# Where weight loads, weight conversions and the second batch's first loads stand in the order of a Fourier filter and mixture-of-experts kernel

## The chip, the cores and the metric

The kernel runs on one core of a Trainium2 chip. The metric is the device time in microseconds (us), lower is better. Three runs of the kernel before took 1503.29, 1506.89 and 1511.69 us, so the median is 1506.89 us.

## The reference

A batch of 8 sequences (2496 x 256, float32) is filtered in the frequency domain, and each of the 19968 filtered rows goes through the one of 8 experts that its router picks:

```python
X = np.fft.rfft(x, axis=1)
y = np.fft.irfft(X * (filt_r + 1j * filt_i)[None], n=2496, axis=1)      # 8 x 2496 x 256
xn = y / (norm(y) + 1e-6);  en = emb / (norm(emb) + 1e-6)               # rows, experts
logits = xn @ en.T / tau;   e = argmax(logits);   gate = softmax(logits)[e]
out = gate * (relu(y @ w1[e]) @ w2[e])                                  # w1: 256 x 1024, w2: 1024 x 256
```

## The kernel before, in words

**The filter.** Each of the 8 batches is a group. Its transform of length 2496 = 64 x 39 is done by matmuls in four steps, each a Python generator: `conv_s1` (products `s1_g_t`, 11 tiles, stored to the DRAM buffer SD), `conv_s2` (loads `a` from SD, products `s2_g_k`, 10 tiles; VectorE multiplies by the filter tiles `f` into `yy` and `xs`, GpSimd adds the two; product `sa_g_j`; store to ZD), and `conv_sb` (loads from ZD, products `y`, 11 tiles, quantised to two float16 halves in `rows`, transposed as `tp`, router logits `lp`). `route` counts ranks with matmuls `rk`, and 22 indirect DMAs per batch (line 767) scatter the rows to the DRAM buffer XS, sorted by expert.

**The slots.** A `Slot` is a block of up to 256 rows of one expert; slot `0_e` is that of batch 0 and expert e. SyncE (SP) loads its rows transposed (`xT`, line 890) and their index and gate (`meta`). Then, for each of four quarters `fp`, `up` runs 12 matmuls into `ph` (line 921), ScalarE (ACT) writes the ReLU as the upper float16 half of `h` (line 927), VectorE (DVE) writes the lower half (line 928), and `down`, two quarters later, runs 12 matmuls into `po` (line 948). There are two buffers for `ph`, so quarter n+2 waits for the lower half of quarter n. A block of 12 matmuls, up or down, is called a block below.

**The weights.** An expert's float32 weights come in four pieces of 128x1024 (w1 in two, w2 in two), loaded by `weight_load`, 1 MB per DMA. Before use DVE takes the maximum of each piece (`wmx`, line 251), two small matmuls (`pm`, lines 262 and 266) with DVE work between make the scale `wsc`, and each piece is scaled and split into two float16 halves: ACT 286 and 287 with GpSimd 288 for the first piece, ACT 290 with DVE 291 for the others. Before slot `0_e` can start, all of w1 of expert e must be converted.

**What sets the order.** The front of the program, through batch 0's router, stands in the order in which it is written. After that, each engine's order is chosen at build time by a list scheduler that goes by its own estimates of time; the engines then run their lists strictly in order. `behind(name)` is the kernel's handle on it: an instruction issued under it may not be placed ahead of the one that `last[name]` holds. Before the change `last` knows "sum", "sp" (the latest slot's `meta` load), "pe" and "dve". The slots of batch g run while `conv_s2` and `conv_sb` of batch g+1 and `conv_s1` of batch g+2 are worked off between their blocks. All the weights are loaded and converted before or during the slots of batch 0.

Of the kernel before, what the change touches and what calls it, by code (L numbers as in the profile page):

```python
# [57 lines left out]
def moe_spectral_kernel(  # L58
# [154 lines left out]

    def weight_load(q, e, j):

        w = (w1, w2)[j]
        if e + 1 < E:
            raw = W32[:, e + 1, j * 2048:(j + 1) * 2048]
            q.dma_start(raw, w[:, e])
            raws[e, j] = [[raw[:, i * 1024:(i + 1) * 1024]] for i in range(2)]  # L220
        elif j == 0:
            raw = W32[:, e, 2048:4096]
            q.dma_start(raw, w[:, e])
            raws[e, j] = [[raw[:, i * 1024:(i + 1) * 1024]] for i in range(2)]
        else:
            raw = W32[:, e, 2048:3072]
            q.dma_start(raw, w[:, e, 1024:2048])
            small = []
            for i in range(2):
                t = mp2.tile([P, 512], F32, tag="wp", name=f"wraw{i}")  # L230
                q.dma_start(t, w[:, e, i * 512:(i + 1) * 512])
                small.append(t)
            raws[e, j] = [small, [raw]]
# [10 lines left out]
    def weight_halves():  # L244
# [3 lines left out]
        def largest(e, j):  # L248
            pieces = raws[e, j][0] + raws[e, j][1]
            for i, r in enumerate(pieces):  # L250
                v.tensor_reduce(out=wmx[:, i:i + 1], in_=r, axis=AX.X, op=ALU.max, apply_absolute_value=True)  # L251
            v.tensor_reduce(out=wmax[:, e, j:j + 1], in_=wmx[:, :len(pieces)], axis=AX.X, op=ALU.max)

        def spread_max(e, js):
# [23 lines left out]
        def halves(e, j):  # L278
            sc = wsc[:, e, j // 2:j // 2 + 1]
            pieces = raws[e, j // 2][j % 2]  # L280
            w = 1024 // len(pieces)
            for i, raw in enumerate(pieces):
                hi = W[:, e, j * 2048 + i * w:j * 2048 + (i + 1) * w]
                lo = W[:, e, j * 2048 + 1024 + i * w:j * 2048 + 1024 + (i + 1) * w]
                if j == 0:
                    nc.scalar.activation(raw, raw, AF.Copy, scale=sc)
                    nc.scalar.copy(hi, raw)
                    nc.gpsimd.tensor_tensor(out=lo, in0=raw, in1=hi, op=ALU.subtract)
                else:
                    nc.scalar.activation(hi, raw, AF.Copy, scale=sc)  # L290
                    v.scalar_tensor_tensor(out=lo, in0=raw, scalar=sc, in1=hi, op0=ALU.mult, op1=ALU.subtract)

        def maxima(e):
# [146 lines left out]
    def load_f(g, k):  # L440
        nb = GROUPS[g]
        fts = []
        for k2 in range(k * 2 // nb, (k + 1) * 2 // nb):
            if g:
                ft = cf.tile([P, 2, D], F32, tag="f", name=f"f{g}_{k2}")
            else:
                ft = W32[:, E - 3:].rearrange("p e c -> p (e c)")[:, k2 * CW:(k2 + 1) * CW]
                ft = ft.rearrange("p (r c) -> p r c", r=2)
            (nc.scalar if g == 1 and k < 2 else nc.sync).dma_start(ft, filt[k2])
            fts.append((k2, ft))  # L450
        return fts

# [26 lines left out]
    def conv_s2(g):  # L479
# [5 lines left out]

        def load_a(k):
            at = cin.tile([P, CW], F32, tag="in", name=f"a{g}_{k}")
            (nc.scalar if g == 1 and k < INB - 1 else nc.sync).dma_start(at, sd[:, k])
            return at

        def filtered(out_, in_, fts, ri):
# [371 lines left out]
    def behind(engine):  # L863
        return tc.issue_after(last[engine].ins) if engine in last else ExitStack()

    class Slot:
# [45 lines left out]
        def up(self, fp, between=None):  # L912
# [4 lines left out]
            for fi in range(2):  # L917
                c = 0
                for k in range(2):
                    for wh, xh in ((0, 0), (0, 1), (1, 0)):  # L920
# [3 lines left out]
                        if between and fi * 6 + c == MID:  # L924
                            between()
            h = mp3.tile([P, 2, 2, 256], F16, tag="h", name=f"h{nm}_{fp}")
            nc.scalar.activation(h[:, 0, :, :size], ph[:, :, :size], AF.Relu)  # L927
            hd = nc.vector.scalar_tensor_tensor(out=h[:, 1, :, :size], in0=ph[:, :, :size], scalar=0.0,  # L928
                                           in1=h[:, 0, :, :size], op0=ALU.max, op1=ALU.subtract)
            self.hs.append(h)  # L930
            if fp == 2:
                gate = self.meta[:, :, 1]
# [229 lines left out]
```

## Time and profile before

| | |
|---|---|
| median of three runs | 1506.89 us |
| time of the profiled execution | 1503.04 us |
| its span, first to last instruction | 1501.3 us |
| mean granted TensorE clock | 0.923 of full |
| TensorE busy | 1299.1 us, 87% |
| VectorE busy | 874.5 us, 58% |
| ScalarE busy | 694.8 us, 46% |
| GpSimd busy | 556.0 us, 37% |

Busy time is the time in which an engine had an instruction at work; it is an average over stages with different limits. The change bears on one stage, from the end of batch 0's router (about 133 us into the span) to the first matmul of batch 1's slots (about 345 us), so the rows further down are read there.

### The profile page before, as it was taken

The numbers are of one execution on the slowest core, as the hardware profiler recorded it, in microseconds if no ns is written. First come the engines' busy times: TensorE is split into PE (matmuls) and PEld (weight loads), VectorE is DVE, ScalarE is ACT, GpSimd is POOL, SyncE is SP. The second block draws the span as 40 slices with busy tenths as digits, with TensorE's granted clock in tenths as the row PEclk, the third lists the DMA queues.
The fourth block names the chain that finished last, engine by engine and source line by source line (L and its number), as shares of the span: only waits on it lengthen the run. The fifth ranks groups of instructions, "written<-read, shape, count | busy, mean of one in ns | idle before, by whom it ended". The sixth has DMA issues, their size and how long they took to land.

```text
span 1501.3 us, 32031 instructions
## 1 busy us (share of the span) xinstructions
PE 1299.1 (87%) x10972; PEld 990.7 (66%) x10972; DVE 874.5 (58%) x2870; ACT 694.8 (46%) x1578; POOL 556.0 (37%) x621
## 2 busy tenths in 40 slices
PE   5563599869898988899989988999899689999998
PEld 2132376546666756686678666867787568899997
DVE  2478967754465746575656555755577342266665
ACT  3451567535544744465346534653466122333333
POOL 1325234443344424542444244524531451122222
PEclk7875699989999999999999998999999889999999
DMA  9778657447756574657466746674664222122221
GB/s 294 252 230 271 201 180 208 137 155 201 186 138 173 178 177 131 183 178 197 129 189 185 190 107 182 182 190 128 182 175 104 77 82 54 42 57 48 48 45 40
DMA packets 229958, 229.15 MB, mean 153 GB/s; under 512 B 125867, under 2 KB 171915, under 8 KB 227870
## 3 DMA queue, kind: packets, MB, share of 16 engines
q1 hardware_dynamic: 199900, 150.10, 37.9%
q0 software_dynamic: 26592, 60.28, 13.0%
q10 hardware_dynamic: 3298, 16.64, 3.2%
q8 instruction: 92, 1.51, 0.4%
q14 instruction: 76, 0.62, 0.1%
HBM read 121.61 MB, written 84.84 MB: 138 GB/s over the span
## 4 chain that ended last, share of the span: by engine, by line
PE 61%; issue 15%; DVE 7%; DMA 7%; ACT 4%; POOL 4%; another core or an unknown queue 2%; SPq 0%; POOLq 0%; ACTq 0%; DVEq 0%
PE ph L921 20%; PE po L948 20%; PE s L431 5%; PE y L431 5%; POOL out_dram L956 3%; PE tp L658 3%; DMA ZD<-z 2%; PE s L436 2%; PE sa L436 2%; DMA f<-ZD 2%; PE sa L431 2%; DVE wmx L251 1%; PE lp L673 1%; DMA in<-in_x 1%
## 5 line engine op out<-in xcount | busy, mean ns | idle before, releaser
L948 PE MATMUL po<-W,h 128*128 128x256 f16 (+1 forms) x3864 | 523.9, 280 | 29.5 <-issue 15.8
L948 PEld LDWEIGHTS <-h 128*128 128x128 f16 x3864 | 376.6, 100 | 135.6 <-issue 83.1
L921 PE MATMUL ph<-xT,W 128*128 128x256 f16 x3072 | 415.1, 281 | 20.2 <-issue 9.3
L928 DVE SCALAR_TENSOR_TENSOR h<-ph,h 128x512 f16<-128x512 f32 (+1 forms) x388 | 231.3, 597 | 270.0 <-ACT h L927 226.8
L921 PEld LDWEIGHTS <-W 128*128 128x128 f16 x3072 | 304.2, 101 | 113.7 <-issue 72.9
L927 ACT ACTIVATE h<-ph 128x512 f16<-128x512 f32 (+1 forms) x388 | 203.2, 526 | 353.0 <-PE ph L921 204.3
L956 POOL DMA_INDIRECT out_dram<-o,meta x161 | 170.0, 1056 | 383.0 <-ACT o L955 329.2
L767 POOL DMA_INDIRECT XS<-rows,ixi x176 | 173.6, 986 | 163.3 <-issue 122.3
L537 POOL TENSOR_TENSOR yy<-yy,xs 128x512 f32<-128x512 f32 x80 | 107.2, 1342 | 205.4 <-DVE xs L500 121.3
L431 PE MATMUL y<-f,csb_sb 120*128 120x512 f32 (+1 forms) x192 | 102.9, 622 | 30.5 <-DMA f<-ZD 29.6
L391 POOL DMA_DIRECT2D in<-in_x x84 | 65.2, 781 | 149.1 <-PE s L431 112.5
L431 PE MATMUL s<-in,c_sb 117*128 117x512 f32 (+1 forms) x192 | 103.4, 634 | 12.2 <-DMA in<-in_x 6.7
L623 ACT ACTIVATE rows<-y 128x256 f16<-128x256 f32 x176 | 66.1, 384 | 91.7 <-PE y L431 85.3
L921 PE MATMUL ph<-xT,wp 128*128 128x128 f16 x1584 | 104.9, 219 | 0.1
L921 PEld LDWEIGHTS <-wp 128*128 128x128 f16 x1584 | 96.6, 98 | 2.8 <-issue 0.3
L474 ACT COPY s<-s 128x512 f32<-128x512 f32 x88 | 51.6, 587 | 99.0 <-PE s L431 45.3
L955 ACT ACTIVATE o<-po,meta 128x256 f32<-128x256 f32 x161 | 69.7, 475 | 56.8 <-PE po L948 33.3
L593 DVE SCALAR_TENSOR_TENSOR rows<-y,rr,rows 128x256 f16<-128x256 f32 x176 | 77.0, 476 | 27.6 <-ACT rows L590 26.1
L909 DVE COPY wp<-W 128x1024 f16 x132 | 62.1, 471 | 46.0 <-PE ph L921 44.1
L590 ACT ACTIVATE rows<-y,rr 128x256 f16<-128x256 f32 x176 | 73.8, 475 | 32.0 <-DVE rr L628 24.9
L498 DVE TENSOR_TENSOR yy<-s,f 128x256 f32<-128x256 f32 x140 | 52.8, 417 | 53.9 <-ACT xs L531 47.6
L658 PEld LDWEIGHTS <-rows 128*128 128x128 f16 x704 | 49.8, 100 | 40.5 <-issue 36.2
(184 smaller groups left out, 1427.5 us busy)
## 6 DMA issues: line engine op xcount, KB each, us to landing
f<-in_filt SPq DMA_DIRECT2D x136, 256.0 KB
ZD<-z SPq DMA_DIRECT2D x80, 256.0 KB
a<-SD SPq DMA_DIRECT2D x77, 256.0 KB
SD<-s SPq DMA_DIRECT2D x80, 240.0 KB
f<-ZD SPq DMA_DIRECT2D x80, 240.0 KB
in<-in_x POOLq DMA_DIRECT2D x70, 234.0 KB
W<-in_w ACTq DMA_DIRECT2D x14, 1024.0 KB
W<-in_filt SPq DMA_DIRECT2D x20, 256.0 KB
```

The costliest lines, as they stand in the source:

```text
L431: nc.tensor.matmul(out_, c[:a.shape[0]], a, start=True, stop=True)
L537: last["sum"] = nc.gpsimd.tensor_tensor(out=yy, in0=yy, in1=xs, op=ALU.add)
L590: nc.scalar.activation(rows[:, i, 0:D], y[:, i], AF.Copy, scale=rr[:, u:u + 1])
L593: nc.vector.scalar_tensor_tensor(out=rows[:, i, D:2 * D], in0=y[:, i], scalar=rr[:, u:u + 1], in1=rows[:, i, 0:D], op0=ALU.mult, op1=ALU.s ...
L658: nc.tensor.transpose(tp[:, i, j], rows[:, i, j * P:(j + 1) * P], ident)
L767: i = nc.gpsimd.indirect_dma_start(out=XS, out_offset=bass.IndirectOffsetOnAxis(ap=ix, axis=0), in_=src, in_offset=None)
L921: last["pe"] = nc.tensor.matmul(ph[:, fi, :size], wp[:, k * 2 + wh, fi * P:(fi + 1) * P], xT[:, xh * 2 + k], start=(c == 0), stop=(c == 5))
L927: nc.scalar.activation(h[:, 0, :, :size], ph[:, :, :size], AF.Relu)
L928: hd = nc.vector.scalar_tensor_tensor(out=h[:, 1, :, :size], in0=ph[:, :, :size], scalar=0.0, in1=h[:, 0, :, :size], op0=ALU.max, op1=ALU. ...
L948: nc.tensor.matmul(self.po[:, s], self.hs[fp][:, hh, fi, s * P:(s + 1) * P], self.Wp[:, off + wh * 1024:off + wh * 1024 + D], start=(fp == ...
L955: nc.scalar.activation(o, self.po[:, s], AF.Copy, scale=self.meta[:, s, 1:2])
L956: i = nc.gpsimd.indirect_dma_start(out=out, out_offset=bass.IndirectOffsetOnAxis(ap=self.meta[:, s, 0:1].bitcast(I32), axis=0), in_=o, in_ ...
```

## The change

Two more instructions are remembered in `last`: each ReLU as "relu" and each lower half as "lower". In the part that the scheduler orders, a weight load on ACT's queue, and the first ACT operation of each converted piece, may no longer be placed ahead of the latest slot's latest ReLU at the point where it is written; the maxima of the weight pieces not ahead of the latest lower half; the last expert's loads on SP, and batch 1's first loads of filter tiles and of SD, not ahead of the latest slot's `meta` load. Batch 1's first four filter loads and first three SD loads move from ACT's queue to SP's.

```diff
@@ -213,6 +213,11 @@
 
     def weight_load(q, e, j):
 
+        with behind("relu" if q is nc.scalar else "sp"):
+            loaded(q, e, j)
+
+    def loaded(q, e, j):
+
         w = (w1, w2)[j]
         if e + 1 < E:
             raw = W32[:, e + 1, j * 2048:(j + 1) * 2048]
@@ -248,7 +253,8 @@
         def largest(e, j):
             pieces = raws[e, j][0] + raws[e, j][1]
             for i, r in enumerate(pieces):
-                v.tensor_reduce(out=wmx[:, i:i + 1], in_=r, axis=AX.X, op=ALU.max, apply_absolute_value=True)
+                with behind("lower"):
+                    v.tensor_reduce(out=wmx[:, i:i + 1], in_=r, axis=AX.X, op=ALU.max, apply_absolute_value=True)
             v.tensor_reduce(out=wmax[:, e, j:j + 1], in_=wmx[:, :len(pieces)], axis=AX.X, op=ALU.max)
 
         def spread_max(e, js):
@@ -283,11 +289,13 @@
                 hi = W[:, e, j * 2048 + i * w:j * 2048 + (i + 1) * w]
                 lo = W[:, e, j * 2048 + 1024 + i * w:j * 2048 + 1024 + (i + 1) * w]
                 if j == 0:
-                    nc.scalar.activation(raw, raw, AF.Copy, scale=sc)
+                    with behind("relu"):
+                        nc.scalar.activation(raw, raw, AF.Copy, scale=sc)
                     nc.scalar.copy(hi, raw)
                     nc.gpsimd.tensor_tensor(out=lo, in0=raw, in1=hi, op=ALU.subtract)
                 else:
-                    nc.scalar.activation(hi, raw, AF.Copy, scale=sc)
+                    with behind("relu"):
+                        nc.scalar.activation(hi, raw, AF.Copy, scale=sc)
                     v.scalar_tensor_tensor(out=lo, in0=raw, scalar=sc, in1=hi, op0=ALU.mult, op1=ALU.subtract)
 
         def maxima(e):
@@ -446,7 +454,8 @@
             else:
                 ft = W32[:, E - 3:].rearrange("p e c -> p (e c)")[:, k2 * CW:(k2 + 1) * CW]
                 ft = ft.rearrange("p (r c) -> p r c", r=2)
-            (nc.scalar if g == 1 and k < 2 else nc.sync).dma_start(ft, filt[k2])
+            with behind("sp" if g == 1 else ""):
+                nc.sync.dma_start(ft, filt[k2])
             fts.append((k2, ft))
         return fts
 
@@ -485,7 +494,8 @@
 
         def load_a(k):
             at = cin.tile([P, CW], F32, tag="in", name=f"a{g}_{k}")
-            (nc.scalar if g == 1 and k < INB - 1 else nc.sync).dma_start(at, sd[:, k])
+            with behind("sp" if g == 1 else ""):
+                nc.sync.dma_start(at, sd[:, k])
             return at
 
         def filtered(out_, in_, fts, ri):
@@ -924,9 +934,10 @@
                         if between and fi * 6 + c == MID:
                             between()
             h = mp3.tile([P, 2, 2, 256], F16, tag="h", name=f"h{nm}_{fp}")
-            nc.scalar.activation(h[:, 0, :, :size], ph[:, :, :size], AF.Relu)
+            last["relu"] = nc.scalar.activation(h[:, 0, :, :size], ph[:, :, :size], AF.Relu)
             hd = nc.vector.scalar_tensor_tensor(out=h[:, 1, :, :size], in0=ph[:, :, :size], scalar=0.0,
                                            in1=h[:, 0, :, :size], op0=ALU.max, op1=ALU.subtract)
+            last["lower"] = hd
             self.hs.append(h)
             if fp == 2:
                 gate = self.meta[:, :, 1]
```

The instructions and their number are the same, apart from the queue of those seven loads. Their order differs from the end of batch 0's router until the first slots of batch 1, and not after. Line numbers of the changed kernel are 5 to 11 higher for the same statement.

**SP's queue at the end of the front.** `s1_10` is the last store of batch 1's first step, `wraw` are pieces of the last expert's w2, `a1` loads of batch 1 from SD, `f1` its filter tiles, `xT0_0` the first slot's rows. Before:

```order
L476 DMA SD1_179<-s1_10_1181 40x256
L231 DMA wraw0_2611<-in_w2 128x512
L231 DMA wraw1_2613<-in_w2 128x512
L488 DMA a1_3_1362<-SD1_179 128x512
L488 DMA a1_4_1405<-SD1_179 128x512
L890 DMA_TRANSPOSE xT0_0_1252<-XS_194 128x4x256
L892 DMA meta0_0_1254<-XS_194 128x2x2
```

And after:

```order
L485 DMA SD1_179<-s1_10_1181 40x256
L900 DMA_TRANSPOSE xT0_0_1252<-XS_194 128x4x256
L902 DMA meta0_0_1254<-XS_194 128x2x2
L458 DMA f1_0_1276<-in_filt 128x512
L458 DMA f1_1_1278<-in_filt 128x512
L458 DMA f1_2_1280<-in_filt 128x512
L458 DMA f1_3_1282<-in_filt 128x512
L498 DMA a1_0_1295<-SD1_179 128x512
```

The first slot's rows now stand ahead of all of `f1`, `a1` and `wraw`, where they stood behind two `wraw` and two `a1`.

**DVE around the first slot's lower halves.** `h0_0_n` on line 928 (938 after) is the lower half of quarter n; `wmx` on line 251 (257 after) is the maximum of a weight piece, 291 a conversion. Before:

```order
L251 TENSOR_REDUCE wmx_177<-W_170 128x1 x2
L274 RECIPROCAL winv_176<-wsc_175 128x2
L291 SCALAR_TENSOR_TENSOR W_170<-W_170,wsc_175 128x1024
L252 TENSOR_REDUCE wmax_172<-wmx_177 128x1
L276 TENSOR_TENSOR isc_171<-winv_176 128x1
L291 SCALAR_TENSOR_TENSOR W_170<-W_170,wsc_175 128x1024
L258 TENSOR_SCALAR wmax_172<-wmax_172 128x2
L251 TENSOR_REDUCE wmx_177<-W_170 128x1 x2
L291 SCALAR_TENSOR_TENSOR W_170<-W_170,wsc_175 128x1024
L928 SCALAR_TENSOR_TENSOR h0_0_0_1269<-ph0_0_0_1256,h0_0_0_1269 128x512
L259 TENSOR_SCALAR wmax_172<-wmax_172 128x2
L928 SCALAR_TENSOR_TENSOR h0_0_1_1345<-ph0_0_1_1301,h0_0_1_1345 128x512
```

And after:

```order
L797 SCALAR_TENSOR_TENSOR bad0_1246<-thr_165,adm0_1244 128x16
L800 TENSOR_SCALAR drop0_1248<-bad0_1246 128x16
L938 SCALAR_TENSOR_TENSOR h0_0_0_1269<-ph0_0_0_1256,h0_0_0_1269 128x512
L257 TENSOR_REDUCE wmx_177<-W_170 128x1 x2
L938 SCALAR_TENSOR_TENSOR h0_0_1_1345<-ph0_0_1_1301,h0_0_1_1345 128x512
L938 SCALAR_TENSOR_TENSOR h0_0_2_1392<-ph0_0_2_1379,h0_0_2_1392 128x512
L945 TENSOR_TENSOR meta0_0_1254<-meta0_0_1254,isc_171 128x2
L258 TENSOR_REDUCE wmax_172<-wmx_177 128x1
L948 TENSOR_TENSOR meta0_0_1254<-meta0_0_1254,drop0_1248 128x2
L257 TENSOR_REDUCE wmx_177<-W_170 128x1 x2
L938 SCALAR_TENSOR_TENSOR h0_0_3_1467<-ph0_0_3_1454,h0_0_3_1467 128x512
L258 TENSOR_REDUCE wmax_172<-wmx_177 128x1
```

Before, 22 maxima and nine conversions on line 291 since the end of the router stand ahead of the first lower half; after, none does. All maxima and conversions of experts 1, 2 and 3 now follow it.

**TensorE around the scale of expert 5.** `pm5_0` on line 266 (272 after) is the second small matmul for expert 5's scale. Before, it stands in the up block of slot `0_3`, two slots ahead of the one that needs it:

```order
L921 MATMUL ph0_3_2_2166<-xT0_3_1860,W_170 128x256
L921 LDWEIGHTS W_170
L921 MATMUL ph0_3_2_2166<-xT0_3_1860,W_170 128x256
L266 MATMUL pm5_0_1797<-wdg_174,one32_144 128x2
L921 LDWEIGHTS W_170
L921 MATMUL ph0_3_2_2166<-xT0_3_1860,W_170 128x256
```

After, it stands in the last down block of slot `0_4`:

```order
L959 MATMUL po0_4_2597<-W_170,h0_4_3_2667 128x256
L272 MATMUL pm5_0_1797<-wdg_174,one32_144 128x2
L959 LDWEIGHTS h0_4_3_2667
L959 MATMUL po0_4_2597<-W_170,h0_4_3_2667 128x256
L959 LDWEIGHTS h0_4_3_2667
L959 MATMUL po0_4_2597<-W_170,h0_4_3_2667 128x256
```

and these rows follow a few matmuls later, with expert 5's own slot already among them:

```order
L272 MATMUL pm6_0_1943<-wdg_174,one32_144 128x2
L439 MATMUL s1_2_0_1971<-in2_0_1963,c1_sb_117 128x512
L439 MATMUL s1_2_1_2048<-in2_1_1965,c1_sb_117 128x512
L931 LDWEIGHTS W_170
L931 MATMUL ph0_5_0_2737<-xT0_5_2416,W_170 128x256
L931 LDWEIGHTS W_170
L931 MATMUL ph0_5_0_2737<-xT0_5_2416,W_170 128x256
L931 LDWEIGHTS W_170
L931 MATMUL ph0_5_1_2837<-xT0_5_2416,W_170 128x256
L931 LDWEIGHTS W_170
L931 MATMUL ph0_5_1_2837<-xT0_5_2416,W_170 128x256
L439 MATMUL y1_0_1955<-f1_0_1897,csb_sb_120 128x512
```

The scale of expert 5 thus moved from two slots ahead of its use to half a block and four products ahead of it, and the first four matmuls of slot `0_5` (those that need no lower weight half) are drawn ahead of `y1_0`. At the end of the stage, the rank matmul `rk1_4` has 87 matmuls of slots `0_6` and `0_7` (27 `ph` and 60 `po`) between it and `rk1_8` before, and none after: they now stand ahead of it. On GpSimd the output stores of slots `0_6` and `0_7` now stand ahead of the scatters that follow `rk1_4` (eight) and `rk1_8` (six); before, only those of `0_5` stood ahead of the eight.

## Rows read from the trace of the kernel before

**Rows 1.** The page: the span, and busy time of TensorE and VectorE.

```profile
span 1501.3 us, 32031 instructions
...
PE 1299.1 (87%) x10972; PEld 990.7 (66%) x10972; DVE 874.5 (58%) x2870; ACT 694.8 (46%) x1578; POOL 556.0 (37%) x621
```

**Rows 2.** Busy time by stretch: from:to, length, each engine, TensorE clock, DMA share, GB/s.

```profile
133.50:165.70 32.20, 5.85 (x21) 2.66 (x22) 30.96 (x78) 11.57 (x12) 14.46 (x15) 0.50 0.94 344
...
165.70:205.80 40.10, 33.78 (x199) 22.88 (x199) 31.17 (x69) 20.81 (x31) 12.62 (x10) 0.85 0.57 157
205.80:250.00 44.20, 42.58 (x305) 30.73 (x304) 29.92 (x59) 33.38 (x59) 23.02 (x21) 1.00 0.66 192
250.00:287.00 37.00, 36.02 (x314) 25.49 (x313) 33.16 (x134) 23.43 (x70) 12.55 (x19) 1.00 0.62 163
287.00:345.00 58.00, 39.73 (x277) 25.34 (x276) 25.37 (x114) 17.36 (x33) 28.79 (x30) 0.82 0.46 144
```

**Rows 3.** SP in order of time: start, length (with waits inside a run), what was issued.

```profile
142.07 19.93 SPq L488 DMA_DIRECT2D a<-SD  x2
162.10 1.35 SPq L890 DMA_TRANSPOSE xT<-XS  x1
...
341.18 1.24 SPq L890 DMA_TRANSPOSE xT<-XS  x1
```

**Rows 4.** Waits of SP's queue, 130 to 170 us: total, times, longest.

```profile
SPq L488 <- PE s L431: 13.0, 1, 13.0
```

**Rows 5.** GpSimd in order of time, in brackets the idle time before.

```profile
146.97 0.90 POOL L767 DMA_INDIRECT XS<-rows,ixi  x1 [0.30 <-issue]
...
235.21 2.44 POOL L288 TENSOR_TENSOR W<-W 128x1024 f16<-128x1024 f32 x1 [3.48 <-ACT W L287]
...
310.20 0.99 POOL L767 DMA_INDIRECT XS<-rows,ixi  x1 [0.30 <-issue]
...
337.40 0.91 POOL L767 DMA_INDIRECT XS<-rows,ixi  x1 [0.30 <-issue]
```

**Rows 6.** TensorE in order of time.

```profile
165.74 5.19 PE L921 MATMUL ph<-xT,W 128*128 128x256 f16 x24 [1.96 <-DMA xT<-XS]
...
204.94 1.02 PE L431 MATMUL s<-a,c_sb 128*128 128x512 f32 x2
...
228.64 0.38 PE L266 MATMUL pm<-wdg,one 2*128 2x2 f32 x2
...
306.67 0.19 PE L738 MATMUL rk<-oh,lt 128*128 128x64 f16 x1
...
344.88 2.56 PE L921 MATMUL ph<-xT,W 128*128 128x256 f16 x22
```

**Rows 7.** VectorE in order of time.

```profile
136.35 2.34 DVE L251 TENSOR_REDUCE wmx<-W 128x1 f32<-128x1024 f32 x2
...
149.97 0.21 DVE L272 TENSOR_SCALAR wsc<-wsc 128x1 f32<-128x1 f32 x2 [0.56 <-DVE wmax L252]
...
178.49 0.68 DVE L928 SCALAR_TENSOR_TENSOR h<-ph,h 128x512 f16<-128x512 f32 x1
```

**Rows 8.** VectorE's maxima from 133 to 165.7 us, grouped: busy, mean ns.

```profile
L251 DVE TENSOR_REDUCE wmx<-W 128x1 f32<-128x1024 f32 x18 | 21.0, 1206 | 0.0
```

**Rows 9.** ScalarE in order of time.

```profile
150.16 1.15 ACT L286 ACTIVATE W<-W,wsc 128x1024 f32<-128x1024 f32 x1 [18.00 <-DVE wsc L272]
...
154.33 1.03 ACT L287 CAST W<-W 128x1024 f16<-128x1024 f32 x1
...
191.04 0.60 ACT L927 ACTIVATE h<-ph 128x512 f16<-128x512 f32 x1 [0.18 <-PE ph L921]
```

**Rows 10.** The chain that ended last, in order of time: start, length, what.

```profile
213.08 1.31 PE ph L921 x12
...
216.02 0.86 PE s L431 x2
...
311.69 8.59 another core or an unknown queue
```

## The prediction

> **What bounds the kernel now.** I read the page first: TensorE is busy 87% of the 1501.3 us span, VectorE 58% [rows 1]. Such a kernel gets faster only where TensorE stands idle, so I cut the stage in which the two orders differ into stretches [rows 2]; the reader is to compare TensorE's and VectorE's columns. From 133.5 to 165.7 us TensorE works 5.85 of 32.20 us while VectorE works 30.96. From 165.7 to 205.8 TensorE has 33.78 of 40.10. From 205.8 to 287 it is nearly full (42.58 of 44.20, 36.02 of 37.00). From 287 to 345 it has 39.73 of 58.00. The hole in front is the prize; the two full stretches are where anything pushed out of the hole must find room; the last stretch is batch 1's router.
>
> Why the hole? SP issues the first slot's rows at 162.10, behind two `a1` loads that held its queue for 19.93 us from 142.07 [rows 3], 13.0 of them for a product on line 431 that had to free the buffer [rows 4]. The first `ph` matmul starts 3.64 us after the issue, at 165.74 [rows 6]. The last scatter, which that load needs, was over at 146.97 + 0.90 = 147.87 [rows 5]. So the rows waited 14 us for their place in a queue. VectorE did not waste the time: it began the first maxima at 136.35 [rows 7], and 18 of them took 21.0 us [rows 8].
>
> **The change, part by part.** I sum against the profiled execution's 1503.04 us.
>
> *A. The rows' load goes ahead of `a1`, `f1` and `wraw`.* In batch 1 the same load is issued at 341.18 [rows 3], the last scatter ending at 337.40 + 0.91 = 338.31 [rows 5]: 2.87 later. The same after 147.87 gives 150.7, plus 3.64 gives a first matmul at 154.4 against 165.74: **-11.3**. The seven loads that go from ScalarE's queue to SP's cost no time of their own as I see it: the DMA engines were 0.94 busy in the hole, 0.57 in the next stretch [rows 2], and the products that need them now come at about 181 (below). Were they later than that, those products would wait and not the rows, which now stand ahead of them.
>
> *B. Maxima behind the first lower half.* 24 matmuls took 5.19 us [rows 6], so the first 12 are over 2.6 after 154.4; the ReLU is 0.60 [rows 9], the lower half 0.68 [rows 7]: 158.3. Expert 1's maxima, which began at 136.35, begin 22.0 us later. Ahead of its scale now stand five pairs of maxima at 2.34 (11.7), two more lower halves (1.4) and the small operations and matmuls of the scale, for which I allow 2.2: about 173.6, against 149.97 [rows 7].
>
> *C. Conversions behind ReLUs.* From the scale, ScalarE took from 150.16 to 155.36 to write its halves [rows 9]: 5.2, so 179; GpSimd's lower half is up to 2.44 more [rows 5]: 181. Slot `0_1` needs all of it for its third matmul; I put that at 182 and the block's ReLU, which also stands behind a conversion for expert 2, at 187. Before, that ReLU came at 191.04 [rows 9]. So of the 11.3 us only 4 are left here. Slot `0_0`, its 96 matmuls done from 154.4, is over at about 167.6, and TensorE then stands idle for some 11 us, apart from a few small matmuls: a new hole in place of the old.
>
> The rest I count in TensorE work done by 205.8, walking the new order with these durations. A slot matmul is 1.31 / 12 = 0.109, a pair of products 0.86 [rows 10]. Before: 175 slot matmuls (19.1) and 11 pairs (9.5), 28.6. After: 205 (22.4) and 7 pairs (6.0), 28.4. So by 205.8 the gain has been paid back: **A + B + C = 0**. Bounds: -11.3 (the preparation never waits) and +6 (the new hole also throws the clock back, below).
>
> *D. VectorE's debt.* It lost 22.0 us of work. Free on it were 1.2 us in the first stretch and 8.9 in the second [rows 2]. So at 205.8 it is 11.9 us behind. From 205.8 to 250 it has 14.3 free, from 250 to 287 only 3.8. The debt fits, but in gaps of which not all can be used, and a late lower half holds back the `ph` buffer. Nothing in the trace prices that; bounds are 0 (all in gaps) and +11.9 (none). I take **+2**, nearer the first, since the free time exceeds the debt.
>
> *E. Expert 5's scale just in time.* Before, `pm5` ran at 228.64 [rows 6], and the first piece's GpSimd half, from 235.21, ended 2.44 later at 237.65 [rows 5]: 9.0 us from matmul to ready weights. In the new order there stand between that matmul and the third of slot `0_5` ten slot matmuls (1.1), four pairs (3.4) and `pm6` at 0.38 and some: 5.1. So TensorE waits up to 3.9; ScalarE may be there a little earlier, so **+3**, bounds 0 and 3.9. Everything else in TensorE's order stands behind that wait.
>
> *F. The end of the stage.* Before, `rk1_4` ran at 306.67 and the first `ph` of batch 1 at 344.88 [rows 6]. After, 27 `ph` and 60 `po` of the last two slots stand ahead of `rk1_4`: 87 x 0.109 to 0.12 = 10 us, so 317 if nothing earlier had moved. From there the path is GpSimd's: 2.2 to the first operation, two stores and 14 scatters, each 0.99 + 0.30 [rows 5], 20.6; then 2.87 to the load; and 344.88 - 341.18 = 3.7 to the matmul: 29.4, so 346.4. That is **+1**. It rests on the patch in which slot matmuls crept, 8.59 us that the chain gives to an unknown queue [rows 10], no longer costing, since the slots are done when the scatters come. If it comes back elsewhere, the term is +8, so bounds 0 and +8.
>
> Sum: 0 + 2 + 3 + 1 = +6, so 1509. The profiled execution is 3.85 us under the median of the three runs (1503.29 to 1511.69); for a median I add half of that: **1511**. One run in three differs from another by 0.5%, so less than 0.5% (7.5 us) I call no change.
>
> **The rivals.**
>
> *The gain stays (faster).* If the preparation is not what slot `0_1` waits for, the 11.3 us stay and D to F fit into gaps: 1503.04 - 11.3 + 2 = 1494. For it: the hole is TensorE's largest. Against: VectorE was 30.96 of 32.20 busy there, with work that has to be done anyway. It decides where expert 1's scale stands before 167 rather than 173.6, or that ReLU before 180.
>
> *VectorE becomes the bound (slower).* None of the 11.9 us of debt finds a gap, since gaps come where VectorE waits for ReLUs: 1503.04 + 11.9 + 3 + 1 + 2 = 1521. For it: the last full stretch has only 3.8 free. Against: the stretch before has 14.3. It decides where VectorE is over 95% busy from 205 to 250 and TensorE falls visibly below 42.58 of 44.20.
>
> *The rows gain nothing.* Were the scatters' data to land late, near 160, the load could not be issued much earlier than 162.10, and the preparation would be late all the same: 11.3 + 6 + 2 on top, 1522. Batch 1's 2.87 us speak against it.
>
> *The clock is paid for twice.* The granted clock was 0.50 in the first stretch and 0.85 in the second, in which TensorE had just begun to work [rows 2]; 24 matmuls took 5.19 there [rows 6], 12 take 1.31 later [rows 10]. The second stretch so lost 0.15 x 40.1 = 6.0 us. If the new hole after slot `0_0` sends the clock down to 1.2 GHz again, that ramp comes once more: 1517. The Trainium skill, "TensorE: Matmul & The Clock Gate", section "What's actually happening", has the low clock as the default state, which activity lifts. By that rule the new hole would cost a ramp of its own, as the first stretch did here; no row shows such a hole in the middle of the slots.
>
> **How the numbers follow.** Forecast (no change, 1511, its own range 1502 to 1515) 0.43; gain stays 0.22; VectorE 0.22; clock 0.08; rows gain nothing 0.05. The forecast's mass above 1514.4 is about 0.05 and below 1499.4 about 0.01, and some of the gain's mass falls within the bound, so faster 0.22, same 0.40, slower 0.38. For the range I reach to the gain at 1494 and past VectorE's case to 1524; half of the gain's chance and a little above are left out.
>
> **What would show it.** A: the rows' load at 151 and the first `ph` near 154. B and C: the first lower half near 158, expert 1's first conversion near 174, TensorE idle from 168 to 179. D: VectorE over 75% from 205 to 287. E: a wait of 3 us inside slot `0_5`'s first block. F: the first `ph` of batch 1, which the two traces share from there on, 6 us later than 344.88. I am wrong if that matmul comes earlier than 340 (the debt found room after all) or later than 352.

## The result, and the profile after

The changed kernel takes 1519.47 us, the median of 20 runs (1508.73 to 1525.67), against 1506.63 us for the kernel before (20 runs, 1499.20 to 1511.69): a ratio of 1.0084, with a 95% interval of 1.0067 to 1.0101. It is slower by 0.84%, some 13 us. The profiled execution has a span of 1518.4 us, 17.1 more than before [rows 1].

Most of that arises in the stage that the prediction looked at. Its trace comes to the start of the stage, the last rank matmul of batch 0's router, 2.6 us later than the trace of before, in a part where the two orders are the same (in all the traces of this document that matmul lies between 133.5 and 136.9 us, and at 134.1 in a second trace of the changed kernel). So some 14 us belong to the stage, close to the 13 of the medians. Before, then after:

```profile
133.45 0.22 PE L738 MATMUL rk<-oh,lt 128*128 128x48 f16 x1 [2.10 <-DVE mv L728]
```

```profile
136.01 0.22 PE L748 MATMUL rk<-oh,lt 128*128 128x48 f16 x1 [2.11 <-DVE ixi L770]
```

The page, and the stage by the same stretches as before [rows 2] (from:to, length, busy time of TensorE, its weight loads, VectorE, ScalarE, GpSimd, then the granted clock, DMA share and GB/s):

```profile
span 1518.4 us, 32037 instructions
...
PE 1308.9 (86%) x10972; PEld 992.8 (65%) x10972; DVE 880.2 (58%) x2870; ACT 694.6 (46%) x1578; POOL 560.3 (37%) x621
```

```profile
133.50:165.70 32.20, 11.56 (x83) 8.87 (x83) 10.62 (x41) 3.12 (x6) 12.10 (x14) 0.58 0.65 146
165.70:205.80 40.10, 25.26 (x144) 15.52 (x141) 38.40 (x71) 24.96 (x32) 14.62 (x8) 0.79 0.79 210
205.80:250.00 44.20, 43.18 (x295) 30.81 (x296) 38.60 (x80) 24.35 (x41) 17.87 (x15) 0.96 0.60 194
250.00:287.00 37.00, 28.45 (x193) 18.34 (x192) 26.65 (x58) 23.82 (x51) 14.78 (x17) 0.91 0.68 196
287.00:345.00 58.00, 46.50 (x392) 32.12 (x391) 40.28 (x197) 26.49 (x67) 25.59 (x32) 0.91 0.44 128
```

In the hole, TensorE has twice its work (11.56 us for 5.85) and VectorE a third (10.62 for 30.96). In the next stretch it is the other way round: VectorE 38.40 of 40.10, TensorE 25.26 for 33.78. Then the surprise: from 250 to 287 us, where both engines were nearly full before, TensorE falls to 28.45 of 37.00 and VectorE to 26.65. In 287 to 345 TensorE catches up (392 matmuls for 277).

The start of the stage: GpSimd's last scatter and SP's load of the rows, then TensorE in order of time (in brackets the idle time before, and what ended it):

```profile
149.50 0.89 POOL L777 DMA_INDIRECT XS<-rows,ixi  x1 [0.30 <-issue]
...
151.67 1.34 SPq L900 DMA_TRANSPOSE xT<-XS  x1
```

```profile
154.93 5.28 PE L931 MATMUL ph<-xT,W 128*128 128x256 f16 x24 [18.53 <-DMA xT<-XS]
...
164.17 3.98 PE L959 MATMUL po<-W,h 128*128 128x256 f16 x35
168.83 0.38 PE L268 MATMUL pm<-ident,wmax 128*2 128x128 f32 x2 [0.67 <-DVE wmax L265]
...
179.64 1.03 PE L931 MATMUL ph<-xT,W 128*128 128x256 f16 x4 [0.63 <-ACT W L294]
182.87 0.59 PE L268 MATMUL pm<-ident,wmax 128*2 128x128 f32 x2 [2.20 <-DVE wsc L278]
183.39 2.07 PE L439 MATMUL s<-a,c_sb 128*128 128x512 f32 x2
185.26 3.15 PE L931 MATMUL ph<-xT,W 128*128 128x256 f16 x17
```

And the place where it loses most, on TensorE and then on ScalarE and GpSimd (line 293 to 295 are the conversion of a first piece, 298 that of the others, 565 the copy of a filter product on its way to ZD):

```profile
252.23 0.38 PE L272 MATMUL pm<-wdg,one 2*128 2x2 f32 x2
...
255.16 0.38 PE L272 MATMUL pm<-wdg,one 2*128 2x2 f32 x2 [0.62 <-DVE wdg L270]
256.66 1.13 PE L439 MATMUL s<-in,c_sb 117*128 117x512 f32 x2 [1.12 <-DVE wsc L273]
258.54 1.13 PE L439 MATMUL s<-in,c_sb 117*128 117x512 f32 x2 [0.75 <-ACT z L565]
259.50 0.60 PE L931 MATMUL ph<-xT,W 128*128 128x256 f16 x4
264.65 2.08 PE L439 MATMUL y<-f,csb_sb 120*128 120x512 f32 x2 [4.55 <-DMA f<-ZD]
266.52 3.47 PE L931 MATMUL ph<-xT,W 128*128 128x256 f16 x17
```

```profile
253.03 1.15 ACT L293 ACTIVATE W<-W,wsc 128x1024 f32<-128x1024 f32 x1 [2.07 <-DVE wsc L278]
254.08 3.21 ACT L298 ACTIVATE W<-W,wsc 128x1024 f16<-128x1024 f32 x3
257.20 0.81 ACT L966 ACTIVATE o<-po,meta 128x256 f32<-128x256 f32 x2
257.91 0.57 ACT L565 COPY z<-sa 128x512 f32<-128x512 f32 x1
258.38 1.05 ACT L294 CAST W<-W 128x1024 f16<-128x1024 f32 x1
...
262.23 2.15 POOL L295 TENSOR_TENSOR W<-W 128x1024 f16<-128x1024 f32 x1
```

Expert 5's scale comes at 252.23, and its weights are whole at 262.23 + 2.15 = 264.38. The last product of the filter's second step, copied at 257.91 behind four conversions, has yet to go through ZD before `y1_0` can start at 264.65. TensorE's idle time in these rows is 0.62 + 1.12 + 0.75 + 4.55 = 7.0 us, and what follows it runs at the lower clock (0.50 granted from 264.5 to 267 us): a pair of `y` in 2.08 us.

The end of the stage:

```profile
333.38 0.19 PE L748 MATMUL rk<-oh,lt 128*128 128x64 f16 x1
...
361.48 2.87 PE L931 MATMUL ph<-xT,W 128*128 128x256 f16 x24
```

Batch 1's first `ph` is 361.48 - 344.88 = 16.6 us later than before [rows 6], and that stays to the end (17.1). Of both, 2.6 us were there at the start of the stage.

### The profile page after: what moved, and what is told of

Its sections match the earlier page's. It is cut to its first block, busy times and chain, and to the rows that moved or that the text cites. A ratio compares the mean times of both kernels' runs of the same rounds, so it can differ in the third digit from the quotient of the medians.

```text
span 1518.4 us, 32037 instructions
## 1 busy us (share of the span) xinstructions
PE 1308.9 (86%) x10972; PEld 992.8 (65%) x10972; DVE 880.2 (58%) x2870; ACT 694.6 (46%) x1578; POOL 560.3 (37%) x621
## 4 chain that ended last, share of the span: by engine, by line
PE 59%; issue 16%; DMA 7%; DVE 6%; ACT 4%; POOL 4%; another core or an unknown queue 2%; SPq 0%; POOLq 0%; DVEq 0%; ACTq 0%
PE ph L931 20%; PE po L959 19%; PE s L439 6%; PE y L439 5%; POOL out_dram L967 3%; PE tp L668 3%; DMA ZD<-z 2%; PE sa L444 2%; PE s L444 2%; DMA f<-ZD 2%; PE sa L439 1%; DVE wmx L257 1%; PE lp L683 1%; DVE W L299 1%
## 5 line engine op out<-in xcount | busy, mean ns | idle before, releaser
L959 PE MATMUL po<-W,h 128*128 128x256 f16 (+1 forms) x3864 | 518.3, 278 | 19.4 <-issue 19.0
L931 PE MATMUL ph<-xT,W 128*128 128x256 f16 x3072 | 419.9, 283 | 35.0 <-DMA xT<-XS 18.5
L439 PE MATMUL s<-in,c_sb 117*128 117x512 f32 (+1 forms) x192 | 107.8, 658 | 15.2 <-DMA in<-in_x 5.5
```

What stands on the lines that cost most here:

```text
L439: nc.tensor.matmul(out_, c[:a.shape[0]], a, start=True, stop=True)
L931: last["pe"] = nc.tensor.matmul(ph[:, fi, :size], wp[:, k * 2 + wh, fi * P:(fi + 1) * P], xT[:, xh * 2 + k], start=(c == 0), stop=(c == 5))
L959: nc.tensor.matmul(self.po[:, s], self.hs[fp][:, hh, fi, s * P:(s + 1) * P], self.Wp[:, off + wh * 1024:off + wh * 1024 + D], start=(fp == ...
```

## The experiments

Two theories were set against each other once this was seen. **Theory 1, the ring**: the `pm` matmuls of the weight scales share a pair of PSUM buffers (pool `ps_c`) with batch 1's filter products, in the order in which they are written: pm1, pm2, pm3, then `s2_1_0`, ..., pm5 between `sa_1_7` and `sa_1_8`. Late maxima so hold back the second batch's filter (its first product at 183.39, at 159.6 before), that makes pm5 late, and the wait at slot `0_5` is the price. **Theory 2, the debt**: VectorE's work of experts 1 to 3 has to be done somewhere; the hole was free for it, and whatever stands there later is late by as much, wherever the wait shows.

Ratios are to the kernel before, run beside them on the same chip, with 95% intervals. That kernel took 1508.92 us (29 runs) beside e1 to e4, 1406.98 (20) beside e5 to e8 and 1507.64 (26) beside e9 to e12, so times are compared within a set only. The ratios are those on record; the quotients of the medians differ from them by up to 0.2% (most for e8 and e12). "Hole" is VectorE's busy time from 133.5 to 165.7 us, of 32.2. "Batch 1's loads" includes those of the last expert on SP's queue, "weight loads" means those on ScalarE's queue. The traces come to the start of the stage up to 3.4 us apart, so smaller differences in the column of the first `ph` mean little.

| run | rules of the change that are left | first `ph` (us) | hole (us) | ratio |
|---|---|---|---|---|
| before | none | 165.7 | 30.96 | 1 |
| e1 | batch 1's loads | 160.4 | 31.20 | 0.9919 (0.9893 to 0.9946) |
| e11 | batch 1's loads, conversions | 160.1 | 30.90 | 0.9969 (0.9945 to 0.9993) |
| e3 | conversions, weight loads | 154.8 | 25.60 | 1.0002 (0.9978 to 1.0025) |
| e8 | all but maxima | 155.6 | 24.23 | 1.0112 (1.0081 to 1.0144) |
| e9 | all (the changed kernel again) | 153.2 | 12.03 | 1.0067 (1.0044 to 1.0090) |
| e12 | all but weight loads | 160.1 | 6.08 | 1.0132 (1.0100 to 1.0164) |
| e2 | maxima | 164.9 | 3.76 | 1.0120 (1.0089 to 1.0151) |
| e4 | all; `pm` in its own buffer | 153.2 | 12.52 | 1.0045 (1.0021 to 1.0070) |
| e5 | all but weight loads; `pm` in its own buffer | 161.6 | 4.81 | 1.0074 (1.0047 to 1.0100) |
| e6 | batch 1's loads; `pm` in its own buffer | 160.2 | 31.34 | 0.9926 (0.9900 to 0.9951) |
| e7 | none; `pm` in its own buffer | 178.0 | 30.77 | 1.0004 (0.9985 to 1.0022) |
| e10 | all; pm5 and pm6 in their own buffer | 153.8 | 11.99 | 1.0067 (1.0041 to 1.0093) |

**e1: batch 1's loads alone.** From the changed kernel:

```diff
-        with behind("relu" if q is nc.scalar else "sp"):
+        with behind("" if q is nc.scalar else "sp"):
-                with behind("lower"):
+                with ExitStack():
-                    with behind("relu"):
+                    with ExitStack():
```

(the last at both conversions). 

> One part of the change alone: batch 1's first loads and the last expert's loads stay behind the first slot's `meta` load on SP, while maxima, conversions and weight loads are as free as before. The order puts the first slot's rows at the head of SP's queue and still eight rows of maxima and six conversions ahead of the first lower half. Theory 1 (the ring: the small `pm` matmuls of a weight scale share their two PSUM buffers, in the order written, with batch 1's filter products, so late maxima hold back that batch's filter): s2_1_0 starts within 6 us of before's 159.6, the 11.3 us of the earlier first slot mostly stay, 1497 us (1493 to 1501). Theory 2 (the debt: VectorE lost 22 us of work): VectorE loses little here, so also faster, about 1497. If the early rows are worth nothing by themselves: 1506.

Measured 1498.22 us, 0.81% faster than before: as both theories have it, and with e6 the best of the kernels by ratio. The first slot is early and VectorE keeps the hole (31.20). In the one profiled execution, of 1503.84 us where the runs reach from 1487.6 to 1509.2, the gain is small (batch 1's first `ph` at 341.3, 3.6 us earlier than before), so the ratio rests on the runs and not on that trace. But the first `ph` comes at 160.4, not 155, and the chain shows why:

```profile
148.38 7.95 DMA XS<-rows,ixi
156.33 0.02 issue
156.34 1.35 SPq L900
```

The last scatter's data land 7.95 us after its issue at 148.38, beside weight loads (DMA share 0.88 in this stretch). In the changed kernel the weight loads are held back (0.65), and from the last scatter's issue at 149.50 to the load of the rows at 151.67 it is 2.2 us. So the rule on the weight loads gives some 5 us of the early start; e9 and e12, which differ by that rule alone, confirm it (153.2 and 160.1).

**e2: the rule on the maxima alone.** The reverse of e1 on the maxima, with loads and conversions as before:

```diff
-        with behind("relu" if q is nc.scalar else "sp"):
+        with ExitStack():
-                    with behind("relu"):
+                    with ExitStack():
-            with behind("sp" if g == 1 else ""):
-                nc.sync.dma_start(ft, filt[k2])
+            with ExitStack():
+                (nc.scalar if g == 1 and k < 2 else nc.sync).dma_start(ft, filt[k2])
```

(the second at both conversions, and the like of the third for `a1`). 

> One part of the change alone: only the maxima are held behind the latest lower half; loads and conversions as before. The order is almost that of the whole change (no maximum ahead of the first lower half, s2_1_0 in slot 0_1, pm5 in the last quarter of slot 0_4). Both theories: the whole loss comes from here, 1518 to 1521 us. If the rules on conversions and loads carry part of the loss, it is below 1514.

1527.59 us, 1.20% slower, above the 1518 to 1521 that both theories gave and by the medians more than the whole change: the loss is there without the other rules. Nothing is gained at the front (first `ph` at 164.9), and VectorE has 3.76 us of work in the hole.

**e3: the rules on conversions and weight loads alone.** From the changed kernel, `behind("lower")` and batch 1's loads undone as above, and the last expert's loads on SP with them (`"sp"` in `weight_load` becomes `""`). 

> One part of the change alone: only weight loads on ScalarE's queue and conversions are held behind the latest ReLU; maxima and batch 1's loads as before. Five rows of maxima and no conversion stand ahead of the first lower half, pm3 and s2_1_0 in the third quarter of slot 0_0. Theory 1: s2_1_0 at about 168 instead of 183, so about half of the loss: 1508 to 1512 us. Theory 2: VectorE keeps ten maxima in the hole and loses about 12 of 22 us: 1511 to 1514.

1507.86 us, no change (1.0002), just below theory 1's 1508 to 1512 and below theory 2's 1511 to 1514. The first `ph` is at 154.8 here, 11 us early, because SP's list happens to have only one `a1` ahead of the rows and the weight loads wait. I take it that the early start pays for the VectorE work lost (5.4 us of the hole); no run parts the two.

**e4: `pm` in its own buffer.** The changed kernel with

```diff
-            pm = ps_c.tile([P, 2, P], F32, tag="c", name=f"pm{e}_{js.start}")
+            pm = (ps_r if 1 <= e <= 6 else ps_c).tile([P, 2, P], F32, tag="r" if 1 <= e <= 6 else "c", name=f"pm{e}_{js.start}")
```

> The changed kernel with the `pm` tiles of experts 1 to 6 in another PSUM pool (the router's, idle at that time) in place of the one they share with the filter products. Still no maximum and no conversion ahead of the first lower half. In the new order s2_1_0 stands in slot 0_0 and pm5 in slot 0_3. Theory 1: the hole after slot 0_0 fills with filter products, the 10 us of waiting at slot 0_5 go, and the time falls by 10 to 20 us, to 1500 to 1509. Theory 2: VectorE starts its maxima just as late and is just as far behind, so 1515 to 1520.

1515.95 us, 0.45% slower: theory 1 misses, theory 2 has it in its range. The products moved early as the order said, but the fourth waited for its data, and the scale of expert 1, behind it in TensorE's list, with it:

```profile
176.07 2.05 PE L439 MATMUL s<-a,c_sb 128*128 128x512 f32 x2 [7.19 <-DMA a<-SD]
178.04 0.58 PE L268 MATMUL pm<-ident,wmax 128*2 128x128 f32 x2
183.66 0.58 PE L272 MATMUL pm<-wdg,one 2*128 2x2 f32 x2 [5.03 <-DVE wdg L270]
```

The trace is that of a run of 1505.8 us, among the fastest of its 12. It left theory 1 an excuse, the collision of `a1` with two weight loads, which e5 takes away.

**e5: the same, with the weight loads free again** (e4 and the first of e1's edits). 

> The run with `pm` in its own buffer, with the weight loads on ScalarE's queue free again, so that they stand ahead of the first slot as before and not behind its ReLUs. In the run before it the filter products stood early in TensorE's order but one waited 7.2 us for an `a1` load that took 18.5 us to land beside two weight loads of 1 MB. Still no maximum ahead of the first lower half. Theory 1 (ring, and loads that collide): the products now run in the hole, 1498 to 1508 us. Theory 2 (VectorE's 22 us of lost work decide): 1513 to 1518, as with the loads late.

1416.34 against 1406.98 us, 0.74% slower. The kernel before took 1507 us when the expectation was written, so its 1513 to 1518 stands for 0.4 to 0.7%: theory 2, at the top of its range. VectorE had 4.81 us of work in the hole, then 39.63 of 40.10 and 42.69 of 44.20.

**e6: e1 with `pm` in its own buffer** (e1's and e4's edits). 

> The kernel with only batch 1's first loads and the last expert's loads behind the first slot's `meta` load, and `pm` of experts 1 to 6 in its own buffer. Maxima stay free, so VectorE loses nothing. Theory 1: the filter products no longer wait for pm3, so up to 8 us below the loads-only kernel's 1498: 1490 to 1497. Theory 2: VectorE's work is the same, so 1498, no change from the loads alone.

1396.83 against 1406.98 us, a ratio of 0.9926 beside e1's 0.9919: the buffer brings nothing. Theory 2.

**e7: the kernel before with `pm` in its own buffer** (e4's edit on the kernel before). 

> The kernel before with `pm` of experts 1 to 6 in its own buffer, and nothing else changed. The order puts filter products of batch 1 into the hole before the first slot, and the first slot's rows far behind in SP's queue (behind a1_7 and f1_7). Theory 1: products gain what the later first slot loses or more: 1498 to 1507 us. Theory 2: VectorE is full in the hole either way, products cannot be multiplied by the filter sooner, and the late first slot costs: 1508 to 1515.

1409.43 against 1406.98 us, no change (1.0004), between what the two theories gave, with the first slot 12 us later: it does not decide. By e4 to e6, theory 1 falls as the main cause: with the buffers parted the loss stays, and where the maxima are early (e6) parting them brings nothing. That the ring carries a part of the loss where the maxima are late is not excluded (see e12).

**e8: all but the rule on the maxima** (from the changed kernel, `behind("lower")` undone). 

> The changed kernel without its rule on the maxima; the rules on loads and conversions stay. Five rows of maxima and no conversion stand ahead of the first lower half; s2_1_0 is in slot 0_0's third quarter, pm5 in the last of slot 0_4. Both theories: most of the loss goes, 1503 to 1510 us. If the loss lies with the late conversions and loads, it stays above 1514.

1425.96 against 1406.98 us, a ratio of 1.0112: both theories miss. VectorE's rows show a loss that neither had:

```profile
165.59 0.67 DVE L938 SCALAR_TENSOR_TENSOR h<-ph,h 128x512 f16<-128x512 f32 x1
176.36 2.35 DVE L257 TENSOR_REDUCE wmx<-W 128x1 f32<-128x1024 f32 x2 [10.10 <-DMA W<-in_w]
```

VectorE is ready for the next expert's maxima at 166, but its weights were only asked for behind the first ReLU, at 158.35, together with batch 1's loads (DMA share 0.90 from 165.7 to 205.8). It waits 10.1 us, and TensorE, whose next block (at 179.49) needs a lower half queued behind those maxima, stands idle for 10.2. In e3, which holds the weight loads too but not batch 1's, VectorE is busy for all of the 10.3 us from 165.7 to 176 and the ratio is 1.0002: it takes the two rules together.

**e9: the changed kernel again.** No edit. 

> The changed kernel once more, as the mark for the runs beside it, since the kernel before took 1509 us in one set of runs and 1407 us in the next. 0.84% (0.67 to 1.01) slower was measured first; expected again 0.7 to 1.0% slower than before.

1519.12 against 1507.64 us, 0.67% slower (0.44 to 0.90), slightly under the band; the intervals of the two overlap.

**e10: pm5 and pm6 in their own buffer** (e4's edit with 5 in place of 1). 

> The changed kernel with `pm` of experts 5 and 6 alone in another PSUM pool. TensorE's order is the same up to the second quarter of slot 0_3; then pm5 stands one and a half slots earlier, and the last filter products stand later (sa_1_9 in slot 0_5, y1_0 at its end). Theory 1 (the wait at slot 0_5, some 7 us of idle TensorE, is a loss of its own): it goes, and the kernel is 0.1 to 0.4% slower than before in place of 0.84%. Theory 2 (the debt: the filter of batch 1, whose last product leads to the router and the scatters, is late whichever way the slots and the products are interleaved): the end of the stage stays where it is, 0.7 to 1.0% slower.

1516.78 us, 0.67% slower, e9's number: theory 2 by the time. pm5 now runs at 230.69, and the wait at slot `0_5` is gone; what the stage has in its place stands in the windows of this run, in the columns of those above:

```profile
165.70:205.80 40.10, 24.78 (x133) 14.44 (x132) 38.38 (x70) 25.11 (x33) 14.61 (x8) 0.83 0.79 215
205.80:250.00 44.20, 40.81 (x290) 29.64 (x290) 43.25 (x86) 30.71 (x45) 17.77 (x13) 0.96 0.52 168
250.00:287.00 37.00, 33.02 (x241) 22.60 (x239) 22.19 (x63) 20.70 (x54) 16.12 (x21) 1.00 0.80 216
```

VectorE is at 43.25 of 44.20 from 205.8 to 250, and TensorE, full before, falls to 40.81. So the wait at slot `0_5` was mainly where the debt showed. But theory 2 also had the end of the stage stay where it is, and in the traces it does not: batch 1's first `ph` comes 3.3 us earlier than in e9 (second row), of which the span keeps 1.0 (1516.6 for 1517.6).

```profile
356.79 2.56 PE L931 MATMUL ph<-xT,W 128*128 128x256 f16 x22
```

```profile
360.13 2.78 PE L931 MATMUL ph<-xT,W 128*128 128x256 f16 x24
```

The intervals of e9 and e10, each a quarter of a per cent to either side, do not exclude that a few us of the wait were a loss of its own.

**e11: batch 1's loads and the conversions** (from the changed kernel, the rules on the maxima and on ScalarE's weight loads undone). 

> The changed kernel without its rules on the maxima and on the weight loads: batch 1's first loads and the conversions alone stay held. In the run without the maxima rule VectorE then waited 10 us (165.6 to 176.4) for a 1 MB weight load that was only issued behind the first ReLU. If that late load made that run 1.1% slower, it is now 0.3 to 0.8% faster than before, like the run with the loads of batch 1 alone. If the late conversions did, 0.5 to 1.1% slower.

1502.99 against 1507.64 us, 0.31% faster: without the rule on the weight loads e8's loss is gone, its ratio of 1.0112 becomes 0.9969 (from one set of runs to another). Beside e1 (0.9919), the rule on conversions costs half a per cent, also across sets, and the intervals just touch.

**e12: all but the rule on the weight loads.** 

> The changed kernel without its rule on the weight loads; maxima and conversions stay behind the first slot. No maximum ahead of the first lower half. If the maxima cost by the work that VectorE loses, 0.6 to 1.0% slower than before, as with the rule. If late weight loads are what costs, within 0.3% of before.

1530.46 against 1507.64 us, a ratio of 1.0132, more than expected. Between e11 and this the only edit is the rule on the maxima, which costs 1.6% (1.0132 over 0.9969), some 25 us. VectorE's hole goes from 30.90 to 6.08, 24.8 us less. With the weight loads held as well (e9) the loss is half, and the first slot starts 6.9 us earlier (153.2 for 160.1).

The ring comes back here. e5 differs from this run by the buffer of `pm` alone, and it has 1.0074 (1.0047 to 1.0100) beside 1.0132 (1.0100 to 1.0164); e4 differs from e9 in the same way, 1.0045 beside 1.0067. So where the maxima are late the shared buffer may carry up to 0.6% itself. The intervals touch or overlap and the sets differ, so this is not shown. What is left without the ring can be read within one set: e5 over e6 is 1.0074 over 0.9926, or 1.5%, and the rules on maxima and conversions are all that lies between them.

## Why the forecast came out as it did

The forecast was 1511 us and no change, and the range to 1524 held the time. The likeliest case did not come: the kernel is slower by 0.84%, which had 0.38, and the rival in which VectorE is the bound, at 1521, was nearest. The prediction's own sign of being wrong came true: batch 1's first `ph` was to come by 352 and came at 361.48. That the range held the time is in part luck, since it had been drawn to take in the VectorE rival, whose mark the changed kernel did not show. The rival in which the gain stays is what e1 does, once VectorE keeps its work in the hole. The mechanism was right in its front part, and what comes after 205.8 us was under-sized.

**A was right.** Rows' load at 151.67 (150.7 forecast), first `ph` at 154.93 (154.4), 10.8 us earlier for 11.3. That the times agree so closely is luck: the trace stands 2.6 us later from the start of the stage, and the load came 1.3 us after the last scatter's end (149.50 + 0.89) in place of 2.87. But it was read as an effect of SP's order alone. e1, e11 and e12 have that order and start at 160; the other half of the gain comes from the weight loads held back, whose data no longer stand beside the scatters'. The rival that the rows gain nothing because the scatters' data land late has its mechanism there (7.95 us), though its size was overstated.

**B and C were right to within 3 us.** These times too carry the 2.6 us. First lower half at 158.31 (158.3), expert 1's first conversion at 174.38 (174), the new hole on TensorE from 168 to 179.64 (168 to 179). The matmuls of slot `0_1` that need the lower half came 3 us later than 182, at 185.26, behind a pair of filter products. By 205.8 TensorE had done 193 slot matmuls and 6 pairs of products where 205 and 7 were forecast: 26.2 us by the prediction's durations, against 28.6 before. It lacks 2.4, no more than the trace was late from the start, so within the stage A + B + C = 0 held.

**The clock's rival came true beside it.** It had 0.08 and 6 us. After the new hole the granted clock is down again, and after the wait near 260 the same. Two windows (from:to, length, the engines as above, clock, DMA share, GB/s):

```profile
183.00:186.00 3.00, 3.00 (x8) 1.19 (x7) 1.66 (x5) 3.00 (x3) 0.00 (x0) 0.50 0.01 3
264.50:267.00 2.50, 2.35 (x5) 1.00 (x6) 2.50 (x3) 1.22 (x3) 2.20 (x3) 0.50 0.98 292
```

A pair of products takes 2.07 and 2.08 us there, for 1.02 at 204.94 before [rows 6]. The Trainium skill, "TensorE: Matmul & The Clock Gate", section "What's actually happening", has the low clock as the default that activity lifts, and these rows agree: behind each of the two the clock is 0.50, 1.2 of 2.4 GHz. What this cost was not parted from the rest.

**E was the first step that failed.** It had TensorE wait "up to 3.9" and took +3. Measured were 7.0 us of idle time, and low-clock matmuls behind it. From pm5 to whole weights it took 264.38 - 252.23 = 12.2 us where 9.0 were taken from before, since two output and filter copies (257.20, 257.91) stood among ScalarE's conversions and GpSimd, with output stores ahead, began its half at 262.23. And a wait that I did not list stood behind it: the last filter product's copy, queued behind four conversions on ScalarE, kept `y1_0` until 264.65, as long as the weights. That is the place; by e10 it is not the main cause, since with the wait gone the time stays.

**D was therefore too small.** The debt was taken at 2 of 11.9 us, "nearer the first, since the free time exceeds the debt". The free time was counted in an order in which VectorE's work was ready early. In the new order it is not ready when VectorE is free: VectorE idles from 250 to 287 (26.65 busy of 37.00) at a time when the conversions and the second filter step hang on one chain through `pm`, ScalarE and ZD. The stage ended 16.6 us late, 2.6 of them from before it began, and the end of F took 1.3 less than forecast; so what D, E, the clock and the patch under F cost came to about 14 where +5 was taken. Idle time of TensorE can be read for E (7.0) and for the patch (4.4); the rest, 2 to 3 by this reckoning, is D and the clock together. That is a split by place and not by cause: with E's wait gone in e10, the time was lost elsewhere. The mark given for the VectorE rival, over 95% busy from 205 to 250 with TensorE falling, was not met by the changed kernel (38.60 of 44.20, TensorE 43.18), but is met by e10 (98%), where the wait at slot `0_5` is out of the way. e12 against e11 prices the rule on the maxima at 1.6%, close to the 24.8 us that it takes from VectorE's hole.

**F was right behind `rk1_4`, and not ahead of it.** From `rk1_4` to batch 1's first `ph`: 361.48 - 333.38 = 28.1 (29.4 forecast). But the term was taken as if the patch of creeping slot matmuls cost nothing any more. Such a patch stands ahead of `rk1_4` now:

```profile
316.39 0.27 PE L931 MATMUL ph<-xT,W 128*128 128x256 f16 x1 [0.31 <-issue]
317.12 0.49 PE L931 MATMUL ph<-xT,W 128*128 128x256 f16 x3 [0.46 <-issue]
318.54 0.60 PE L931 MATMUL ph<-xT,W 128*128 128x256 f16 x4 [0.93 <-issue]
319.95 0.38 PE L931 MATMUL ph<-xT,W 128*128 128x256 f16 x2 [0.82 <-issue]
322.22 2.07 PE L439 MATMUL s<-in,c_sb 117*128 117x512 f32 x2 [1.89 <-DVE yT L670]
```

That is 4.4 us of idle time on the way to `rk1_4`; the prediction had named the case and bounded it by +8.

What the runs show is that the rule on the maxima is what costs: it is the only edit between e11 and e12 (1.6%), and e2 has the loss with that rule alone. That it costs by the work that VectorE loses in the hole is argued. For it: VectorE is busier from 165.7 to 250 us in the runs with late maxima (69.7 to 82.3 of 84.3 us, 61.1 before), and the loss stays with the ring parted (e5). Against a simple price per us: 24.8 us of the hole go with some 25 us of time from e11 to e12, but 27.2 with 18 from before to e2, and from e8 to e9 the same rule takes 12.2 us from the hole and the ratio falls (1.0112 to 1.0067). That late maxima also make all that hangs on them late, the scales and conversions, was not parted from VectorE's load by any run.

## What to carry to other kernels

An idle TensorE is no prize if the engine that feeds it is busy in that hole: price first what that engine did there, and where it will do it instead. Free time counted on an engine later is worth something only if its work is ready then, so a debt of one engine is better not set off against the sum of its gaps: here the whole debt, 11.9 us, would have come nearer than the 2 us taken. When a change bundles several rules, each moves what the others meet: here one rule alone gained 0.8% (e1), three together cost 1.3% (e12), and the fourth gave half of that back (e9).

## What the hardware showed that was not expected

The same kernel took 1507 to 1509 us in three sets of runs and 1407 us in one, that of e5 to e8, and all the others moved with it; e1 to e4, at 1509, ran on the same chip as that set. The page of e7, from the faster set, shows one difference that answers to a part of it: TensorE's idle time before `po`, by group (busy, mean ns, then idle time before it and what ended most of it), is 2.2 us. The page of the kernel before has 29.5, more than half of it with "issue" as the releaser, that is, nothing that the profile shows. The pages of the slower sets have 16.2 to 29.5 there, those of the faster one 0.1 to 2.2.

```profile
L948 PE MATMUL po<-W,h 128*128 128x256 f16 (+1 forms) x3864 | 499.6, 273 | 2.2 <-ACT o L955 1.6
```

```profile
L948 PE MATMUL po<-W,h 128*128 128x256 f16 (+1 forms) x3864 | 523.9, 280 | 29.5 <-issue 15.8
```

What is short in those patches is not shown by any run. The mean granted clock was also higher there (0.942 for 0.923). A difference of some 27 us in idle time leaves most of the 100 us open. Ratios between kernels are told above within one set, and that they carry over from one to the other is an assumption where e8 is set beside e3, e9 or e11, e6 beside e1, e1 beside e11, and e5 or e4 beside e12 or e9.
